# A fused attention and SwiGLU kernel: two pairs of heads transposed by DMA instead of TensorE

## The chip, the core and the metric

The kernel runs on one core of one Trainium2 chip. A core has a matrix engine (TensorE, "PE" in the profile; its weight loads are "PEld"), a vector engine (VectorE, "DVE"), an activation engine (ScalarE, "ACT"), a general engine (GpSimd, "POOL") and a queue engine (SyncE, "SP"). Each has its own instruction stream, and semaphores tie the streams together. Transfers run on 16 DMA engines; here GpSimd issues those that convert fp32 to fp16, and SyncE issues the others, the transposing ones among them. The metric is the device time of one execution in microseconds.

## The reference

Attention with a local window and a few global keys, followed by a gated feed-forward block. There are 4 batches, 8 heads, 768 positions and 64 values per head. Each query sees the first 8 keys and the last 96 keys up to itself.

```python
scores = scale * np.matmul(q, k.transpose(0, 1, 3, 2))
keep = is_global | is_local                 # first 8 keys, or 0 <= row - col < 96
scores = scores + bias[None, :, :, :]       # -slope of the head * distance
scores = np.where(keep, scores, -1000000000.0)
a = np.exp(scores - max); a = a / (sum(a) + 1e-09)
attn = np.matmul(a, v)                      # (4, 8, 768, 64)

x = attn.transpose(0, 2, 1, 3).reshape(3072, 512)
g = x @ w_gate                              # 512 x 1536
out = (g * sigmoid(g) * (x @ w_val)) @ w_out   # 1536 x 512
```

## The kernel before

The kernel works in fp16 with fp32 sums. A pair is two heads: four pairs in each batch, `hp` 0 to 3. A quad is two pairs: `g` 0 and 1. The feed-forward block runs over 8 tiles of 384 tokens, two for each batch; a tile has 12 steps `f`, one per 128 columns of the inner size. In each step there are four gate matmuls, four value matmuls and some output parts of three matmuls each (`out_part`; four parts make one 128 x 512 block of the output of the tile before). The attention of the coming batch is woven between these steps on TensorE.

For the scores, q and k have to lie with the head's 64 values on the partitions. Batch 1 gets this from TensorE:

```python
def transposes(self):                         # class Pair; batch 1, all four pairs
    trq, trk = (t[:, 0:S] for t in banks("trs", FP16))
    for st, tr in ((kst[b], trk), (qst[b], trq)):
        for j in range(J):                    # 6
            for hi in range(2):
                nc.tensor.transpose(...)      # 24 in all for a pair
    ...
    nc.scalar.copy(out=k3[...], in_=t3[...])  # two, PSUM to kT
    nc.vector.tensor_copy(out=self.qT..., in_=trq...)
    nc.vector.tensor_copy(out=k3[:, :, 0:NG], ...)   # the global keys, in every chunk
```

Batches 2 and 3 get it from DMA. Their q and k are loaded as rows (a position on each partition), the 8 global keys are put into partitions 0 to 7, and SyncE issues transposing transfers:

```python
def transposes_dma(self):
    for dst, st in ((self.kT[:, 0:S], kst), (self.qT, qst)):
        nc.sync.dma_start_transpose(out=..., in_=...)

def load_rows(b, i, h):                       # one head of q or k, on GpSimd's queue
    nc.gpsimd.dma_start(out=..., in_=src[b, h, 0:n * J].rearrange("(t p) d -> p t d", p=n))

def load_ends(b):                             # the last 48 keys of all heads, into kend
def turn_ends(b):                             # kE <- kend, one transposing transfer
    nc.sync.dma_start_transpose(out=kE, in_=kend[b].rearrange("p h d -> p (h d)"))
```

`kend` and `kE` have one buffer each. The seventh chunk of keys is read from `kE` where it was made by DMA.

The weighted values of a quad, and the scaling that gives x:

```python
def values(self, half, bank, mul_eng):        # class Quad; batch 1, first half
    den = bank("den"); self.weigh(half, den, None)
    for side in range(2):
        num = bank("num"); self.weigh(half, num, side)
        src = sb2.tile([128, TB], FP32, name="ns", tag="ns", bufs=4)
        nc.scalar.copy(out=src, in_=num[:, 0:TB])
    def scale_num(side):                      # xT block = ns * rb
        eng = mul_eng if side else nc.vector
        eng.tensor_mul(self.x_out(half, side), srcs[side], self.rb)
    def spread():
        self.spread()                         # rb <- dR
        if mul_eng is nc.gpsimd:
            scale_num(1)
    later.append(lambda: self.invert(den))    # dT <- den, dR <- dT, on VectorE
    later.append(spread)
    ...                                       # then scale_num for what is left
```

Entries of `later` are emitted one by one between the steps. A tile's gate and value products read four x blocks `xT[:, c, :]`, where block c is that of quad c // 2 and side c % 2.

The loads in GpSimd's stream, and the order of the steps in tile 1:

```python
stage(1)
load_qk(1, 0, 4)                              # pairs 0 and 1
load_globals()
load_wo(3)
load_qk(1, 4, 8)                              # pairs 2 and 3
for c in range(NCH):                          # V of batch 1, 7 chunks
    load_v_rest(1, c)
...
def va(b, g, half):
    return lambda: quads[b, g].values(half, bank, nc.vector)

def first(t, b):                              # (t, f): after step f; (t, f, n): before output part n
    return {(t, 2): [tr(b, 0), tr(b, 1)],
            (t, 4): [sc(b, (0, 0), (0, 1), (1, 0))],
            (t, 5): [tr(b, 2), tr(b, 3)],
            (t, 6): [sc(b, (1, 1), (2, 0), (2, 1))],
            (t, 8): [sc(b, (3, 0), (3, 1))],
            (t, 9): [va(b, 0, 0)],
            (t, 10, 1): [va(b, 1, 0), lambda: run_later(len(later))]}
...
# output parts after each step of tile 1, then tile 7
(ff(1, 0, 6, (1, 0, 0, 1, 1, 2)) + ff(1, 6, 10, (1, 1, 1, 0)) + ff(1, 10, 12, (2,)), first(1, 1)),
(ff(7, 0, 10, (1,)) + ff(7, 10, 12), {})
```

Of the kernel before, what the change touches and what calls it, by code (L numbers as in the profile page):

```python
# [10 lines left out]
FP16 = mybir.dt.float16  # L11
# [26 lines left out]
def kernel(  # L38
# [24 lines left out]
    J = S // 128  # L63
    NCH = 7
# [26 lines left out]
    sb2 = ctx.enter_context(tc.tile_pool(name="sb2", bufs=2))  # L91
# [62 lines left out]

    def stage_rows(b):
        qst[b] = sb2.tile([128, NP, J, 2, D], FP16, name="qst", tag="qst")
        kst[b] = sb2.tile([128, NP, J, 2, D], FP16, name="kst", tag="kst")
        kend[b] = sb2.tile([128, H, D], FP16, name="kend", tag="kend", bufs=1)
        nc.gpsimd.memset(kend[b], 0.0)
        nc.sync.dma_start(out=kend[b][0:NG], in_=kG[:, b - 1])  # L160
        for hp in range(NP):
            pair = kG[:, b - 1, 2 * hp:2 * hp + 2, :].rearrange("p h d -> p (h d)")
            nc.sync.dma_start(
                out=kst[b][0:NG, hp].rearrange("p t e d -> p t (e d)"),
                in_=pair.unsqueeze(1).broadcast_to([NG, J, 2 * D]))
# [17 lines left out]
    def copy_globals(b, c0=0):  # L183
        nc.sync.dma_start(
            out=vSs[b][0:NG, c0:],
            in_=vG[:, b, :, :].unsqueeze(1).broadcast_to([NG, NCH - c0, H, D]))


    def load_rows(b, i, h):
        st, src = ((qst, q), (kst, k))[i]  # L190
        p0, n = ((0, 128), (NG, KC))[i]
        nc.gpsimd.dma_start(  # L192
            out=st[b][p0:p0 + n, h // 2, :, h % 2, :],
            in_=src[b, h, 0:n * J].rearrange("(t p) d -> p t d", p=n))
# [58 lines left out]
    later = []  # L253

    def run_later(n):
        for _ in range(n):
            if later:
                later.pop(0)()

    class Pair:  # L260
# [114 lines left out]
        def scores(self, bk, mul_eng, sc):  # L375
            hp = self.hp
            for c in range(NCH):
                cb, col, q0, n = chunks[c]
                if cb != bk:
                    continue  # L380
                for hi in range(2):
                    r = slice(64 * hi, 64 * hi + 64)
                    keys = (kE[r, hp, :] if c == J and self.b > 1
                            else self.kT[r, 128 * c:128 * c + 128])
                    nc.tensor.matmul(  # L385
                        sc[hi][:, col:col + n], lhsT=keys,
                        rhs=self.qT[r, q0:q0 + n], start=True, stop=True)
            at = sb2.tile([128, 2, BANK], FP16, name="at", tag=f"at{bk}", bufs=NP)
            self.at[bk] = at

            def exps():
                for hi in range(2):
                    nc.scalar.activation(out=at[:, hi, :], in_=sc[hi][:, 0:BANK],  # L393
                                         func=AF.Exp, scale=scale)

            def mask():
                m = masks[:, 2 * hp:2 * hp + 2, :]
                if bk == 1:
                    for i in range(2):
                        a2 = at[:, :, WIN * i:WIN * i + WIN]  # L400
                        mul_eng.tensor_mul(a2, a2, m[:, :, WIN:2 * WIN])  # L401
                else:
                    o = WIN // 2 * bk
                    mul_eng.tensor_mul(at, at, m[:, :, o:o + BANK])  # L404

            return exps, mask

        def transposes_dma(self):
            b, hp = self.b, self.hp
            self.qT = sb2.tile([128, S], FP16, name="qT", tag="qT", bufs=NP)  # L410
            self.kT = kTs[hp]
            for dst, st in ((self.kT[:, 0:S], kst), (self.qT, qst)):
                nc.sync.dma_start_transpose(
                    out=dst.rearrange("r (t p) -> r t p", t=J),
                    in_=st[b][:, hp].rearrange("p t e d -> p (t e d)"))


    class Quad:
# [191 lines left out]
    quads = {(b, g): Quad(b, g) for b in range(B) for g in range(2)}  # L610
# [84 lines left out]
    load_qk(1, 0, 4)  # L695
    load_globals()
    load_wo(3)
    load_qk(1, 4, 8)
    for c in range(NCH):
        load_v_rest(1, c)  # L700

    gv["n"] = 1
    hb = [bank("gps") for _ in range(4)]
# [5 lines left out]
    def sc(b, *units):  # L709
        def step():  # L710
            for i, (hp, bk, *other) in enumerate(units):
                pair = pairs[b + 1 if other else b, hp]
                on_vector = pair.b < 2 or bk < 2 or hp % 2 == 0
                exps, mask = pair.scores(
                    bk, nc.vector if on_vector else nc.gpsimd,
                    [spare("sc") for _ in range(2)] if i == 0 and len(units) == 3
                    else banks("sc"))
                if i == 0:
                    exps()
                else:  # L720
                    later.append(exps)
                later.append(mask)
        return step

    def va(b, g, half):
        return lambda: quads[b, g].values(half, bank, nc.vector)

    def vas(b, half):
        return lambda: both_values(b, half)
# [1 line left out]
    def tr(b, hp):  # L731
        return pairs[b, hp].transposes
# [23 lines left out]
    def fetch(b, *hps):  # L756
        def step():
            for hp in hps:
                pairs[b, hp].transposes_dma()
            if hps[0] > 0:  # L760
                turn_ends(b)
        return step

    def first(t, b):
        return {(t, 2): [tr(b, 0), tr(b, 1)],
                (t, 4): [sc(b, (0, 0), (0, 1), (1, 0))],
                (t, 5): [tr(b, 2), tr(b, 3)],
                (t, 6): [sc(b, (1, 1), (2, 0), (2, 1))],
                (t, 8): [sc(b, (3, 0), (3, 1))],
                (t, 9): [va(b, 0, 0)],  # L770
                (t, 10, 1): [va(b, 1, 0), lambda: run_later(len(later))]}

    def both(t, b):

# [35 lines left out]
    def ff(t, f0, f1, n_out=(0,)):  # L810
        return [(t, f, n_out[(f - f0) % len(n_out)]) for f in range(f0, f1)]

    stretches = [
        (ff(0, 9, 10) + ff(0, 10, 12, (1,)), {}),
        (ff(1, 0, 6, (1, 0, 0, 1, 1, 2)) + ff(1, 6, 10, (1, 1, 1, 0)) + ff(1, 10, 12, (2,)), first(1, 1)),
        (ff(2, 0, 12, (1,)) + ff(3, 0, 12, (1,)), both(2, 1)),
        (ff(4, 0, 12, (1,)) + ff(5, 0, 12, (1,)), both(4, 2)),
        (ff(6, 0, 12, (1,)), second(6, 3)),
        (ff(7, 0, 10, (1,)) + ff(7, 10, 12), {})]

    loads, after = {}, {}
# [11 lines left out]
    for b, base, rate, v_at in ((2, 20, 2.0, (31, 32, 33, 34, 35, 36, 37)), (3, 38, 1.4, (56, 57, 58, 59, 60, 61, 62))):  # L833
# [105 lines left out]
```

The softmax here doesn't subtract the row's maximum and nothing guards it: scores larger than these inputs give would overflow.

## Time and profile before

| | before |
|---|---|
| median of 3 runs | 240.92 us (240.61 to 241.65) |
| span of the profiled run | 239.1 us |
| TensorE busy | 232.8 us (97%) |
| VectorE busy | 168.0 us (70%) |
| ScalarE busy | 127.7 us (53%) |
| GpSimd busy | 93.9 us (39%) |

In the page's busy table an engine is followed by its busy microseconds, the share of the span and the number of instructions. The slices divide the span into 40 equal parts of 5.98 us; a digit is the busy share in tenths, and 9 means 90% or more. In a list of waits a line gives who waited, for whom, the sum in us, how often, and the longest. In a timeline or a chain in order of time a line begins with the start in us and the duration in us. In the list of groups the columns are the line, the engine, the operation with its output and inputs, the shapes, the count, then busy us with the mean ns of one, then the engine's idle time before them and what ended it. "L272" is line 272 of the kernel before. SPq is SyncE's queue.

### The profile page before, as it was taken

What the parts mean: (1) busy time and instruction counts of PE and PEld (TensorE: products, weight loads), DVE (VectorE), ACT (ScalarE), POOL (GpSimd) and SP (SyncE); (2) the same over time, 40 slices, a digit from 0 to 9 for tenths busy, and PEclk for the clock granted to TensorE, in tenths of its full rate; (3) what the DMA queues carried; (4) which work ended last, traced back from release to release, by engine and by line L of the source; (5) the groups of instructions that cost most, each with busy time, mean ns of one, the idle gap of its engine ahead of it and who ended that gap; (6) DMA issues with size and microseconds to landing.
All of it is one profiled execution on the core that took longest, in us unless ns stands there. A gap on an engine that the chain in (4) does not pass through costs nothing.

```text
span 239.1 us, 6040 instructions
## 1 busy us (share of the span) xinstructions
PE 232.8 (97%) x2424; PEld 134.9 (56%) x2424; DVE 168.0 (70%) x363; ACT 127.7 (53%) x290; POOL 93.9 (39%) x113
## 2 busy tenths in 40 slices
PE   7899999999999999999999999999999999999994
PEld 4565565656555556555655556555655556555543
DVE  6889569978897678676885668776785668555530
ACT  4836776888846365367346365367356435233311
POOL 8976674568970003994082163700031213000000
PEclk9999999999999999999999999999999999999999
DMA  7999999999999446999149649920110110111022
GB/s 140 161 198 201 181 205 204 195 170 154 157 138 135 111 112 91 126 129 122 41 62 112 112 111 133 127 55 2 46 44 3 44 44 3 47 45 44 7 84 88
DMA packets 83332, 25.00 MB, mean 105 GB/s; under 512 B 72600, under 2 KB 80360, under 8 KB 83304
## 3 DMA queue, kind: packets, MB, share of 16 engines
q0 software_dynamic: 64208, 14.05, 64.2%
q1 hardware_dynamic: 18664, 10.36, 17.8%
q8 instruction: 19, 0.31, 0.5%
q10 hardware_dynamic: 432, 0.21, 0.4%
q14 instruction: 9, 0.07, 0.1%
HBM read 28.62 MB, written 6.29 MB: 146 GB/s over the span
## 4 chain that ended last, share of the span: by engine, by line
PE 85%; DMA 10%; POOL 3%; issue 1%; ACT 0%; POOLq 0%
PE ops L585 25%; PE gps L553 25%; PE vps L553 24%; DMA wg<-in_moe_w_gate_dram 10%; PE num L445 3%; PE sc L385 3%; PE den L445 2%; PE trs L272 1%; POOL vS L169 1%; PE ops L601 1%; POOL k L118 1%; POOL q L118 1%; POOL wg L211 0%; POOL vS L613 0%; ACT osb L605 0%
## 5 line engine op out<-in xcount | busy, mean ns | idle before, releaser
L564 ACT ACTIVATE th<-gps 128x384 f32<-128x384 f32 x96 | 47.3, 494 | 63.1 <-PE gps L553 57.3
L569 DVE SCALAR_TENSOR_TENSOR sl<-th,gps 128x384 f32<-128x384 f32 x96 | 52.7, 551 | 38.6 <-ACT th L564 38.0
L553 PE MATMUL gps<-xT,wg 128*128 128x384 f16 x384 | 78.2, 327 | 0.5 <-DVE xT L503 0.3
L553 PE MATMUL vps<-xT,wv 128*128 128x384 f16 x384 | 77.9, 326 | 0.2 <-DMA wv<-in_moe_w_val_dram 0.2
L585 PE MATMUL ops<-wo,hT 128*128 128x512 f16 x276 | 73.1, 379 | 0.0
L573 DVE TENSOR_TENSOR hT<-vps,sl 128x384 f16<-128x384 f32 x96 | 53.0, 554 | 8.2 <-PE vps L553 0.5
L553 PEld LDWEIGHTS <-wg 128*128 128x128 f16 x384 | 35.5, 98 | 32.1 <-issue 2.1
L553 PEld LDWEIGHTS <-wv 128*128 128x128 f16 x384 | 37.1, 98 | 25.6 <-DMA wv<-in_moe_w_val_dram 0.7
L585 PEld LDWEIGHTS <-hT 128*128 128x128 f16 x276 | 26.9, 98 | 23.6
L393 ACT ACTIVATE at<-sc 128x432 f16<-128x432 f32 x72 | 33.8, 534 | 10.2 <-PE sc L385 10.2
L522 POOL TENSOR_TENSOR xT<-ns,rb 128x384 f16<-128x384 f32 x10 | 9.8, 996 | 65.2 <-DVE rb L461 54.3
L169 POOL DMA_DIRECT2D vS<-in_v_dram x28 | 24.7, 891 | 5.5 <-DMA qst<-in_q_dram 1.4
L591 ACT ACTIVATE osb<-ops 128x512 f32<-128x512 f32 x23 | 13.7, 597 | 14.6 <-PE ops L585 14.4
L404 POOL TENSOR_TENSOR at<-at,masks 128x864 f16<-128x864 f16 x4 | 7.3, 1824 | 23.9 <-ACT at L393 19.3
L404 DVE TENSOR_TENSOR at<-at,masks 128x864 f16<-128x864 f16 x20 | 12.2, 609 | 5.6 <-ACT at L393 5.6
L192 POOL DMA_DIRECT2D kst<-in_k_dram x16 | 14.0, 897 | 2.2 <-PE sc L385 1.5
L518 ACT COPY ns<-num 128x384 f32<-128x384 f32 x24 | 9.8, 494 | 9.6 <-PE num L445 9.6
L192 POOL DMA_DIRECT2D qst<-in_q_dram x16 | 13.7, 883 | 0.9 <-DMA qst<-in_q_dram 0.6
L367 ACT ACTIVATE at<-sc 128x432 f16<-128x432 f32 (+2 forms) x32 | 11.4, 460 | 2.5 <-PE sc L356 2.5
L401 DVE TENSOR_TENSOR at<-at,masks 128x432 f16<-128x432 f16 x24 | 8.1, 377 | 4.4 <-ACT at L393 4.4
L445 PE MATMUL num<-at,vS 128*32 128x216 f16 (+6 forms) x576 | 10.9, 224 | 0.0
L455 DVE STREAM_TRANSPOSE dT<-den 128x384 f32<-128x384 f32 x16 | 9.3, 581 | 1.2 <-PE den L445 0.5
(71 smaller groups left out, 165.8 us busy)
## 6 DMA issues: line engine op xcount, KB each, us to landing
out_dram<-osb SPq DMA_DIRECT2D x23, 256.0 KB
vS<-in_v_dram POOLq DMA_DIRECT2D x24, 120.0 KB, 5.6
wg<-in_moe_w_gate_dram POOLq DMA_DIRECT2D x6, 256.0 KB, 7.7
wv<-in_moe_w_val_dram POOLq DMA_DIRECT2D x6, 256.0 KB, 8.1
wo<-in_moe_w_out_dram POOLq DMA_DIRECT2D x4, 384.0 KB, 10.3
qst<-in_q_dram POOLq DMA_DIRECT2D x16, 96.0 KB, 5.2
kst<-in_k_dram POOLq DMA_DIRECT2D x16, 90.0 KB, 5.6
kst<-in_k_dram POOLq DMA_DIRECT2D x2, 384.0 KB, 11.9
```

Of the source, the lines that this page charges most:

```text
L169: nc.gpsimd.dma_start(out=vSs[b][NG:NG + n, c, :, :], in_=v[b, :, KC * c:KC * c + n, :].rearrange("h p d -> p h d"))
L192: nc.gpsimd.dma_start(out=st[b][p0:p0 + n, h // 2, :, h % 2, :], in_=src[b, h, 0:n * J].rearrange("(t p) d -> p t d", p=n))
L367: nc.scalar.activation(out=at[:, hi, 0:col + n], in_=sc[hi][:, 0:col + n], func=AF.Exp, scale=scale)
L393: nc.scalar.activation(out=at[:, hi, :], in_=sc[hi][:, 0:BANK], func=AF.Exp, scale=scale)
L404: mul_eng.tensor_mul(at, at, m[:, :, o:o + BANK])
L445: nc.tensor.matmul(dst[r, o:o + n], lhsT=ones[:, 0:32] if side is None else vals[:, 4 * g + j, side::2], rhs=pairs[b, 2 * g + j // 2].at[c ...
L553: nc.tensor.matmul(gv[f, which][:, 0:TB], lhsT=w[:, c, 128 * f:128 * f + 128], rhs=x_of(t)[:, c, :], start=(c == 0), stop=(c == NC - 1))
L564: nc.scalar.activation(out=th, in_=dst[:, 0:TB], func=AF.Tanh, scale=0.5)
L569: nc.vector.scalar_tensor_tensor(out=sl, in0=th, scalar=1.0, in1=dst[:, 0:TB], op0=AluOp.add, op1=AluOp.mult)
L573: nc.vector.tensor_mul(hTs[t][:, f, :], dst[:, 0:TB], gv.pop(("sl", f)))
L585: nc.tensor.matmul(ops, lhsT=hTs[t][:, f, 128 * i:128 * i + 128], rhs=wo[:, f, :], start=(f == 0), stop=(f == NFF - 1))
L591: nc.scalar.mul(out=osb, in_=ops, mul=0.5)
```

## The change

Pairs 2 and 3 of batch 1 are transposed by DMA, as those of batches 2 and 3 are; pairs 0 and 1 stay on TensorE. For this their q and k are loaded as rows, one load for each head, and the first four chunks of V are issued between the rows of pair 2 and those of pair 3. The last three chunks of V are issued in tile 2. The steps behind the scores of pair 1 come one step later in tile 1. One output part moves from tile 7 to tile 1. In the first half of batch 1's values, GpSimd scales one of the two x blocks of a quad and VectorE the other. The change is meant to take work off TensorE and off the engines that emptied the transposes' PSUM banks. Helpers are renamed so that both ways can share one staging tile.

```diff
-    load_qk(1, 4, 8)
-    for c in range(NCH):
-        load_v_rest(1, c)
+    stage_ends(1)                       # kend: memset on GpSimd
+    for hp in range(2, NP):
+        for i in (1, 0):
+            for e in range(2):
+                load_rows(1, i, 2 * hp + e)
+        if hp == 2:
+            for c in range(4):
+                load_v_rest(1, c)
+    load_ends(1)
 ...
-        return lambda: quads[b, g].values(half, bank, nc.vector)
+        return lambda: quads[b, g].values(half, bank, nc.gpsimd)
 ...
-            if hps[0] > 0:
+            if hps[-1] == NP - 1:
                 turn_ends(b)
 ...
         return {(t, 2): [tr(b, 0), tr(b, 1)],
-                (t, 4): [sc(b, (0, 0), (0, 1), (1, 0))],
-                (t, 5): [tr(b, 2), tr(b, 3)],
-                (t, 6): [sc(b, (1, 1), (2, 0), (2, 1))],
-                (t, 8): [sc(b, (3, 0), (3, 1))],
-                (t, 9): [va(b, 0, 0)],
-                (t, 10, 1): [va(b, 1, 0), lambda: run_later(len(later))]}
+                (t, 4): [sc(b, (0, 0), (0, 1), (1, 0)), fetch(b, 2)],
+                (t, 5): [fetch(b, 3)],
+                (t, 7): [sc(b, (1, 1), (2, 0), (2, 1))],
+                (t, 9): [sc(b, (3, 0), (3, 1))],
+                (t, 10): [va(b, 0, 0)],
+                (t, 11, 1): [va(b, 1, 0), lambda: run_later(len(later))]}
 ...
-        (ff(1, 0, 6, (1, 0, 0, 1, 1, 2)) + ff(1, 6, 10, (1, 1, 1, 0)) + ff(1, 10, 12, (2,)), first(1, 1)),
+        (ff(1, 0, 6, (1, 0, 0, 1, 1, 2)) + ff(1, 6, 12, (1, 1, 1, 1, 1, 3)), first(1, 1)),
 ...
-        (ff(7, 0, 10, (1,)) + ff(7, 10, 12), {})]
+        (ff(7, 0, 12, (1, 1, 1, 0)), {})]
 ...
+    at_step(1, 0, lambda: rows_globals(1, 2))
     at_step(1, 7, lambda: [copy_globals(b) for b in range(1, B)])
+    at_step(2, 4, lambda: [load_v_rest(1, c) for c in range(4, NCH)])
-    ... batch 2's V chunks at steps (31, 32, 33, 34, 35, 36, 37)
+    ... batch 2's V chunks at steps (34, 35, 36, 37, 38, 39, 40)
```

(Cuts are marked by "..."; the last two lines shorten one long line of the kernel. Steps there are counted through the tiles, 12 to a tile. The cut parts are the renaming, and that the seventh chunk of keys is read from `kE` for pairs 2 and 3 of batch 1 too.)

More of the change, by code (lines that the diff above doesn't have):

```diff
@@ L155, in stage_rows, with stage_ends, rows_of, rows_globals @@
     def stage_rows(b):
-        qst[b] = sb2.tile([128, NP, J, 2, D], FP16, name="qst", tag="qst")
-        kst[b] = sb2.tile([128, NP, J, 2, D], FP16, name="kst", tag="kst")
+        stage(b)
+        stage_ends(b)
+        rows_globals(b, 0)
+    def stage_ends(b):
         kend[b] = sb2.tile([128, H, D], FP16, name="kend", tag="kend", bufs=1)
         nc.gpsimd.memset(kend[b], 0.0)
+    def rows_of(st, b, hp):
+        return st[b][:, 2 * hp:2 * hp + 2, :].rearrange("p h x -> p (h x)").rearrange(
+            "p (t e d) -> p t e d", e=2, d=D)
+    def rows_globals(b, hp0):
         nc.sync.dma_start(out=kend[b][0:NG], in_=kG[:, b - 1])
-        for hp in range(NP):
+        for hp in range(hp0, NP):
             pair = kG[:, b - 1, 2 * hp:2 * hp + 2, :].rearrange("p h d -> p (h d)")
             nc.sync.dma_start(
-                out=kst[b][0:NG, hp].rearrange("p t e d -> p t (e d)"),
+                out=rows_of(kst, b, hp)[0:NG].rearrange("p t e d -> p t (e d)"),
                 in_=pair.unsqueeze(1).broadcast_to([NG, J, 2 * D]))
@@ L192, in load_rows @@
         nc.gpsimd.dma_start(
-            out=st[b][p0:p0 + n, h // 2, :, h % 2, :],
+            out=rows_of(st, b, h // 2)[p0:p0 + n, :, h % 2, :],
             in_=src[b, h, 0:n * J].rearrange("(t p) d -> p t d", p=n))
@@ L382, in scores @@
                     r = slice(64 * hi, 64 * hi + 64)
-                    keys = (kE[r, hp, :] if c == J and self.b > 1
+                    keys = (kE[r, hp, :] if c == J and (self.b > 1 or hp > 1)
                             else self.kT[r, 128 * c:128 * c + 128])
@@ L414, in transposes_dma @@
                     out=dst.rearrange("r (t p) -> r t p", t=J),
-                    in_=st[b][:, hp].rearrange("p t e d -> p (t e d)"))
+                    in_=rows_of(st, b, hp).rearrange("p t e d -> p (t e d)"))
     class Quad:
@@ L831 @@
         mask_at(t, f, n % 2, n // 2, *((0, WIN), (WIN, 3 * WIN))[n % 2])
+    at_step(1, 0, lambda: rows_globals(1, 2))
     at_step(1, 7, lambda: [copy_globals(b) for b in range(1, B)])
-    for b, base, rate, v_at in ((2, 20, 2.0, (31, 32, 33, 34, 35, 36, 37)), (3, 38, 1.4, (56, 57, 58, 59, 60, 61, 62))):
+    at_step(2, 4, lambda: [load_v_rest(1, c) for c in range(4, NCH)])
+    for b, base, rate, v_at in ((2, 20, 2.0, (34, 35, 36, 37, 38, 39, 40)), (3, 38, 1.4, (56, 57, 58, 59, 60, 61, 62))):
         items = [(base, lambda b=b: stage_rows(b)), (base + 1, lambda b=b: load_ends(b))]
```

## The prediction

> **What bounds the kernel now.** I read the page first: busy shares, then the slices.
>
> ```profile
> PE 232.8 (97%) x2424; PEld 134.9 (56%) x2424; DVE 168.0 (70%) x363; ACT 127.7 (53%) x290; POOL 93.9 (39%) x113
> ...
> PE   7899999999999999999999999999999999999994
> ...
> PEclk9999999999999999999999999999999999999999
> DMA  7999999999999446999149649920110110111022
> ```
>
> TensorE is busy 97% of 239.1 us at full clock, and from the fourth slice on no slice is below 90%. A modelled busy share can hide pauses, so next I read who waited for whom on TensorE alone. All its listed waits come to 2.9 us, and all of them lie in the first part of the run:
>
> ```profile
> PE warm L621 <- DVE ones L126: 1.2, 1, 1.2
> PE trs L298 <- DMA q<-in_q_dram: 1.0, 2, 0.7
> PE gps L553 <- DVE xT L503: 0.3, 1, 0.3
> ```
>
> Third, TensorE's own timeline through tile 1: four-matmul groups start every 0.65 us without a gap. So the kernel is bound by the number of TensorE instructions, and only two things can move the time here: taking matmuls out, or making TensorE wait. The chain of work that ended last in order of time prices what goes:
>
> ```profile
> 53.01 1.29 PE ops L585 x6
> 54.30 1.46 PE trs L272 x48
> 55.77 0.76 PE gps L553 x4
> ```
>
> The 48 transposes of pairs 2 and 3 hold TensorE for 1.46 us (30 ns each), and the gate group after them takes 0.76 instead of 0.65.
>
> **What the Trainium skill says.** "TensorE: Matmul & The Clock Gate", Part 4: PE-mode transpose, says such a transpose lands in PSUM and needs a copy afterwards. The trace agrees: two vector copies of 0.95 us (L284) and ScalarE copies of 1.63 us (L280) follow each block. "DMA: Bandwidth & Descriptors", Issuing engines are not separate DMA queues, says transfers from all issuing queues interleave on the same 16 DMA engines; here the DMA line shows them 90% full in the slices where the new transposes must run. "PSUM — Partial Sum Buffer", Engine vs sequencer instructions, calls GpSimd's queue strictly FIFO; the trace agrees, every load and scaling starts in program order. "SBUF — State Buffer", SBUF: two separate sides, says a GpSimd operation and a vector operation with two SBUF inputs exclude each other for a whole instruction. The trace hints at it: the pair of vector scalings at 122.39 us takes 1.17 us where it overlaps GpSimd's scaling, but 1.03 us in the stretch after 200.92 us where the overlap is small.
>
> **Part 1, the transposes removed.** 1.46 + (0.76 - 0.65) = 1.57 us off TensorE. Two qT copies and two kT copies (about 2.2 us of VectorE with the small ones) and 1.63 us of ScalarE also go, in the stretch where VectorE is fullest (61.9 to 73.9 us). Output parts only move: one from tile 7 to tile 1, none added. With no new wait: 240.92 - 1.57 = 239.35 us.
>
> **Part 2, do pairs 2 and 3 arrive in time?** Their q and k now come as eight row loads of 90 or 96 KB in 256-byte source runs, in place of two loads of 384 KB. The GpSimd order of the new program is wo, memset, four row loads (pair 2), V chunks 0 to 3, four row loads (pair 3), ends. In the run before, the last wo was issued at 35.36 and landed 11.7 us later, at 47.1; the six full V chunks behind landed 1.0 us apart (issue plus landing: 52.0 to 57.1). One V chunk has 8 x 120 = 960 runs, a row load 720 to 768, so I estimate 0.8 us each. Pair 2 lands at 47.1 + 4 x 0.8 = 50.3; four V chunks bring 54.4; pair 3 lands at 57.6, and with some 1.5 us for the outputs and transposes that share the engines at 59. A DMA transpose holds its queue 1.2 to 1.3 us:
>
> ```profile
> 85.36 1.98 SPq L413 DMA_TRANSPOSE kT<-kst  x1
> 87.50 1.21 SPq L413 DMA_TRANSPOSE qT<-qst  x1
> 88.88 1.21 SPq L413 DMA_TRANSPOSE kT<-kst  x1
> 90.25 1.21 SPq L413 DMA_TRANSPOSE qT<-qst  x1
> 91.52 1.26 SPq L202 DMA_TRANSPOSE kE<-kend  x1
> ```
>
> Pair 2 is turned by about 54, pair 3 by about 61. When needed: after the outputs at 53.01 the gates of step 6 now start at 54.30; each step with one output part costs 1.95, so pair 2's scores come at 58.2 and pair 3's at about 63. Margins of 4 and 2 us: no wait expected. V's global rows wait on the same queue behind kE (61.3) and an output, so they land near 64; they are needed near 66.
>
> **Part 3, x for tile 2.** I expect the new wait here. The vector work before tile 2 was just in time before:
>
> ```profile
> 69.04 0.58 DVE L455 STREAM_TRANSPOSE dT<-den 128x384 f32<-128x384 f32 x1
> 69.66 0.23 DVE L456 RECIPROCAL dR<-dT 128x12 f32<-128x12 f32 x1
> 69.92 0.58 DVE L461 STREAM_TRANSPOSE rb<-dR 128x384 f32<-128x384 f32 x1
> 70.60 1.03 DVE L481 TENSOR_TENSOR xT<-ns,rb 128x384 f16<-128x384 f32 x2
> 71.55 0.55 DVE L569 SCALAR_TENSOR_TENSOR sl<-th,gps 128x384 f32<-128x384 f32 x1
> ```
>
> x was ready at 71.6 and tile 2's first gate group started at 71.44, whose fourth matmul needs the last x at 71.9. Between quad 1's numerators (end 68.2) and that group lay 3.25 us: an output part, step 11's two products, two output parts. In the new order quad 1 comes inside step 11, and only two output parts follow: 1.3 us. Let step 11's gates start at 0 (66.5 us on the clock). The outer groups then give: products 1.4, an output 0.65, denominators and numerators 0.9, two outputs 1.3, so tile 2's first gate starts at 4.3 and uses its four x blocks at 4.3, 4.45, 4.6, 4.75. VectorE: sl at 1.37 (as 82.08 to 83.45 shows), then rb, hT, x at steps of 0.41, 0.49, 0.44 and dT 0.46 later, at 3.2 (spacings of 66.78 to 69.04); dT to finished rb is 1.46, so 4.6. Then GpSimd scales one block in 1.0 us:
>
> ```profile
> L522 POOL TENSOR_TENSOR xT<-ns,rb 128x384 f16<-128x384 f32 x10 | 9.8, 996 | 65.2 <-DVE rb L461 54.3
> ```
>
> That ends at 5.75, 1.0 us after it is needed. If GpSimd and VectorE exclude each other, quad 0's vector scaling is held up 0.6 us and the final pair runs one after the other, up to 2.3 us late. I take 1.5.
>
> **Part 4, GpSimd's order.** The memset of kend for batch 2 must wait for kE of batch 1, since they share one buffer. Before, batch 2's rows were issued from 51.9; now from about 62. Nine loads at 0.85 fill GpSimd to about 70, and only then come the scalings, wanted at 68.9 and 71.2. So the first may be a little late; each us by which kE finishes after 62 also delays tile 2. Estimate: 0.3 us on average. Batch 2's first pairs land near 75, turned by 80, needed near 83; V chunks 4 to 6 land near 86, needed near 91. No wait.
>
> **Sum.** -1.57 + 1.5 + 0.3 = +0.2 us by this working. I choose 240.7 rather than 241.1: the part of 1.5 that rests on exclusion has only a 0.14 us hint in the trace.
>
> **Rivals.** (a) Everything is hidden: 239.3 us. For it: VectorE has lost some 3 us of work in this stretch, and GpSimd takes half of the scaling. Against: only 1.3 us of TensorE work is left behind quad 1. (b) The DMA side is late. The engines are already full from 48 to 58 us and I add small runs and five transposes there. If pair 3 lands 3 us later, its scores wait 1 us, V's global rows a similar time, and GpSimd reaches the scalings 2 to 3 us later: 242.5 to 244. Against: the last three V chunks leave that stretch. (c) GpSimd becomes the bound of tile 2's start, by the memset's wait alone: 241.5 to 242.5.
>
> **Range and chances.** Rival (a) sets the floor, 239.2. Working plus a 1 us delay of kE gives 242.1; I put the upper end at 242.5. To gain 2% would take 4.8 us, three times what is removed: 0.01. To lose 2%, new waits of 6.4 us: only (b) at its worst, 0.04. Within 2%: 0.95.
>
> **What would show each step.** Right: 48 fewer transposes and TensorE busy about 1.5 us less; no wait of the scores for the transposes; a TensorE wait of 1 to 2 us at the first gates of tile 2 for xT from POOL or DVE; batch 2's row loads issued from about 62. Wrong: no wait at tile 2 (a); a TensorE wait for kT, qT or vS near 58 to 66 (b); kE after 64 and GpSimd's first scaling after 72 (c). A wait later than 80 us for batch 2's kT or V would overturn Part 4.

## The result and the profile after

The changed kernel takes 248.58 us (median of 4 runs, 248.21 to 249.22), the kernel before 240.76 beside it: a ratio of 1.032, 95% interval 1.0283 to 1.0357. The prediction was 240.7 with a range up to 242.5.

On the page of the changed kernel, the busy shares and the slices (6.16 us each here):

```profile
PE 235.3 (96%) x2376; PEld 135.2 (55%) x2376; DVE 166.6 (68%) x357; ACT 125.8 (51%) x286; POOL 102.7 (42%) x123
...
PE   8899999999979969999999999999999999999994
...
PEclk9999999999997997999999999999999999999999
DMA  8999999999999995199917749690110110111022
```

TensorE has 48 instructions fewer and is busy 2.5 us longer. Two things are new in the slices: two dips of PE, and right at them two dips of the granted clock. The list of waits of TensorE names the first:

```profile
PE sc L394 <- DMA qT<-qst: 3.0, 2, 2.4
PE gps L562 <- DVE xT L490: 1.5, 1, 1.5
...
PE gps L562 <- POOL xT L490: 0.5, 1, 0.5
```

TensorE's timeline tells where they lie (the bracket is the idle time before, and what ended it):

```profile
59.07 0.55 PE L394 MATMUL sc<-qT,kT 64*128 64x216 f16 x8 [0.56 <-DMA qT<-qst]
...
71.55 0.49 PE L562 MATMUL gps<-xT,wg 128*128 128x384 f16 x2
73.58 0.32 PE L562 MATMUL gps<-xT,wg 128*128 128x384 f16 x1 [1.55 <-DVE xT L490]
74.42 0.32 PE L562 MATMUL gps<-xT,wg 128*128 128x384 f16 x1 [0.52 <-POOL xT L490]
...
91.06 0.36 PE L394 MATMUL sc<-qT,kT 64*128 64x216 f16 x4 [2.45 <-DMA qT<-qst]
```

So there are three places: pair 2 of batch 1 (0.56), the start of tile 2 (1.55 + 0.52, with 0.27 of idle time before 71.55), and pair 1 of batch 2 (2.45), in tile 2, whose scores the change doesn't touch. The windows behind the last two show the second effect; the columns are the stretch, its us, the busy time (and count) of PE, PEld, DVE, ACT and POOL, the granted clock, the time that DMA packets took as a mean of 16 engines, and GB/s:

```profile
74.90:78.80 3.90, 3.90 (x29) 1.94 (x27) 1.53 (x3) 1.82 (x4) 3.90 (x6) 0.56 1.16 73
91.20:95.70 4.50, 4.50 (x20) 2.08 (x17) 1.63 (x3) 2.18 (x5) 0.00 (x0) 0.62 1.08 184
```

The clock is at half for 3.41 us each time, from 75.08 and from 92.14 on, 0.7 and 1.1 us after TensorE resumes. The loss is (1 - 0.56) x 3.90 = 1.72 and (1 - 0.62) x 4.50 = 1.71 us.

Now a ledger. The denominators at step 8 of tile 2 start at 90.73 us before and at 98.98 after; one output part more (0.65) is done by then, so the changed kernel has lost 7.60 us up to there, and the spans differ by 7.3 in all.

| Term | us |
|---|---|
| transposes gone: from the outputs to step 6's gates, 52.85 to 55.70 before, 52.87 to 54.17 after | -1.55 |
| wait for qT, batch 1 pair 2 | 0.56 |
| start of tile 2 (0.27 + 1.55 + 0.52) | 2.34 |
| wait for qT, batch 2 pair 1 | 2.45 |
| half clock, twice | 3.43 |
| sum, of 7.60 measured | 7.23 |

The rest, 0.37, lies in how the waits are counted: a listed idle time is 0.2 to 0.3 us shorter than the delay that it makes here. From group start to group start, as in the first row, the three waits cost 0.74, 2.62 and 2.62 and the half clock 1.57 and 1.68, and the sum is 7.68. What made the waits is read from three other engines. SyncE's timeline, the transposes that those two waits for qT were for:

```profile
53.06 1.31 SPq L422 DMA_TRANSPOSE qT<-qst  x1
...
83.42 1.84 SPq L422 DMA_TRANSPOSE qT<-qst  x1
```

The first was issued at 53.06 and let the scores go at 59.07: 6.0 us. The second took from 83.42 to 91.06: 7.6 us. Before, the same transpose of batch 2 was issued at 78.16 and no packet moved from 82 to 84, so it took at most 3.8. GpSimd's timeline:

```profile
61.81 0.52 POOL L162 MEMSET kend<- 128x512 f16 x1 [9.15 <-DMA kE<-kend]
...
70.01 1.06 POOL L490 TENSOR_TENSOR xT<-ns,rb 128x384 f16<-128x384 f32 x1
73.00 1.37 POOL L490 TENSOR_TENSOR xT<-ns,rb 128x384 f16<-128x384 f32 x1 [1.94 <-DVE rb L470]
74.32 1.79 POOL L201 DMA_DIRECT2D kst<-in_k_dram  x2
...
81.12 2.56 POOL L178 DMA_DIRECT2D vS<-in_v_dram  x3
```

Behind the memset, row loads fill the engine to 69.96; then come the two scalings, and the other row loads and V of batch 2 stand behind them and are issued from 74.32 to 83.7. Batch 2's transposes are issued from 78.08 to 85.3, so both run together. And VectorE's timeline before tile 2:

```profile
69.79 1.70 DVE L490 TENSOR_TENSOR xT<-ns,rb 128x384 f16<-128x384 f32 x1
...
72.96 0.56 DVE L490 TENSOR_TENSOR xT<-ns,rb 128x384 f16<-128x384 f32 x1
```

One block of scaling takes 0.56 at 72.96, and 1.70 at 69.79: there GpSimd's scaling ran from 70.01 to 71.07. GpSimd's second scaling took 1.37 instead of 1.0, beside VectorE's of 72.96. The transposition that leads to quad 1's x (dT) came behind the 1.70, at 71.42.

### The profile page after: what moved, and what is told of

The parts are those of the page before. It is cut to its first block, busy times and chain, and to the rows that moved or that the text cites. A ratio compares the mean times of both kernels' runs of the same rounds, so it can differ in the third digit from the quotient of the medians.

```text
span 246.4 us, 5972 instructions
## 1 busy us (share of the span) xinstructions
PE 235.3 (96%) x2376; PEld 135.2 (55%) x2376; DVE 166.6 (68%) x357; ACT 125.8 (51%) x286; POOL 102.7 (42%) x123
## 4 chain that ended last, share of the span: by engine, by line
PE 84%; DMA 8%; DVE 3%; POOL 2%; issue 1%; ACT 1%; POOLq 0%; DVEq 0%; ACTq 0%
PE gps L562 25%; PE vps L562 24%; PE ops L594 22%; DMA qT<-qst 5%; PE sc L394 3%; PE num L454 3%; DMA q<-in_q_dram 2%; PE den L454 2%; PE sc L354 1%; PE ops L610 1%; PE sc L365 1%; DVE sl L578 1%; POOL k L118 1%; DVE xT L490 1%; DVE xT L512 1%
## 5 line engine op out<-in xcount | busy, mean ns | idle before, releaser
L562 PE MATMUL gps<-xT,wg 128*128 128x384 f16 x384 | 79.2, 329 | 2.5 <-DVE xT L490 1.5
L594 PE MATMUL ops<-wo,hT 128*128 128x512 f16 x276 | 74.5, 385 | 0.0
L402 ACT ACTIVATE at<-sc 128x432 f16<-128x432 f32 x72 | 33.2, 540 | 5.8 <-PE sc L394 5.8
L201 POOL DMA_DIRECT2D kst<-in_k_dram x20 | 17.5, 888 | 1.7 <-DMA wo<-in_moe_w_out_dram 1.6
L201 POOL DMA_DIRECT2D qst<-in_q_dram x20 | 17.1, 875 | 2.2 <-DMA wo<-in_moe_w_out_dram 1.1
L394 PE MATMUL sc<-qT,kT 64*128 64x216 f16 (+2 forms) x148 | 9.7, 259 | 3.0 <-DMA qT<-qst 3.0
```

Of the source, the lines that this page charges most:

```text
L201: nc.gpsimd.dma_start(out=rows_of(st, b, h // 2)[p0:p0 + n, :, h % 2, :], in_=src[b, h, 0:n * J].rearrange("(t p) d -> p t d", p=n))
L394: nc.tensor.matmul(sc[hi][:, col:col + n], lhsT=keys, rhs=self.qT[r, q0:q0 + n], start=True, stop=True)
L562: nc.tensor.matmul(gv[f, which][:, 0:TB], lhsT=w[:, c, 128 * f:128 * f + 128], rhs=x_of(t)[:, c, :], start=(c == 0), stop=(c == NC - 1))
L594: nc.tensor.matmul(ops, lhsT=hTs[t][:, f, 128 * i:128 * i + 128], rhs=wo[:, f, :], start=(f == 0), stop=(f == NFF - 1))
```

## The experiments

**The theory.** (1) A DMA transpose takes 6 us and more beside loads. (2) GpSimd's scalings stand in its own stream of loads, so they push batch 2's loads onto batch 2's transposes and, by exclusion, delay VectorE's scaling. (3) Waits of about 2 us cost as much again through the clock. **The rivals.** The memset of `kend` behind `kE` is what pushes the loads late, and GpSimd's scaling is harmless; or the transposes are late because of their place in SyncE's stream; or quad 1's late place in tile 1 explains the start of tile 2 alone. The part of (2) on the loads came only after the first four runs: the expectations of those blame exclusion for the scaling's cost and the memset for the late loads.

The medians of the kernel before, on the same chips: 240.62 us for the first four rows, 240.70 for the next four, 240.74 for the next three and 240.84 for the last. The ratio is estimated from the single runs and is not always the quotient of the medians.

| Run | us | ratio to before (95%) |
|---|---|---|
| changed kernel, scaling on VectorE | 242.38 | 1.0111 (1.0041 to 1.0181) |
| changed kernel, two kend buffers | 252.54 | 1.049 (1.0442 to 1.0538) |
| changed kernel, with useless matmuls | 247.15 | 1.0253 (1.0182 to 1.0323) |
| kernel before, GpSimd scaling alone | 244.01 | 1.0157 (1.01 to 1.0214) |
| changed kernel, all rows before the scalings | 245.74 | 1.0146 (1.0057 to 1.0236) |
| scaling on VectorE, quads early | 245.23 | 1.0172 (1.0099 to 1.0246) |
| one pair by DMA | 244.09 | 1.0125 (1.0067 to 1.0184) |
| kernel before, V loads beside the transposes | 247.16 | 1.0237 (1.0179 to 1.0296) |
| quads early, batch 2's scores later | 242.03 | 1.0055 (1.003 to 1.0081) |
| one pair, two kend buffers | 241.19 | 1.0024 (1.0008 to 1.0039) |
| the same, batch 2's scores later | 241.92 | 1.0042 (1.0025 to 1.0059) |
| both pairs, everything later | 241.28 | 1.0016 (1.0001 to 1.0031) |

**Scaling back on VectorE**, in the changed kernel:

```diff
-        return lambda: quads[b, g].values(half, bank, nc.gpsimd)
+        return lambda: quads[b, g].values(half, bank, nc.vector)
```

> The changed kernel, with batch 1's first-half x scaled by VectorE alone (GpSimd's half undone). Theory: GpSimd's scaling and VectorE's scaling of two on-chip inputs exclude each other, which held VectorE's first scaling for 1.2 us and GpSimd's second for 0.4 us. Without it the last x block comes some 1.0 us sooner, at about 73.4, the wait at tile 2 falls from 2.1 to 1.2-1.6 us, and the time to about 247.5; 246 if the wait gets too short to halve the clock. Rival: the late x comes from the place of quad 1 alone (two output parts behind it); then VectorE alone, with one more scaling per quad, is as late or later and the time is 248.6 or more. The wait of 2.4 us for batch 2's qT stays in both.

242.38 us, 1.8 above the kernel before, where the changed kernel is 7.8 above it: 6 us are back, more than the theory gave. The scalings gone, GpSimd's loads run on from 61.84 to 79 almost without a pause, and those that came from 74.32 on in the changed kernel are issued 4.6 to 5 us earlier; the wait for batch 2's qT is 0.63 instead of 2.45. The wait at tile 2 is 1.11, and in the profiled execution no stretch inside the kernel has half the clock (another run of it, 245.14 us, had a mean clock of 0.991). So one line of the change holds most of the loss. Why it is so much, the next runs had to tell.

**A second buffer for kend**, so that batch 2's rows needn't wait for `kE`:

```diff
-        kend[b] = sb2.tile([128, H, D], FP16, name="kend", tag="kend", bufs=1)
+        kend[b] = sb2.tile([128, H, D], FP16, name="kend", tag="kend", bufs=2)
```

> The changed kernel, with two buffers for kend in place of one, so that batch 2's memset and row loads no longer wait for batch 1's kE. Theory: the waits for batch 2's kT and qT (2.4 us, then 3.5 us at half clock) come from its rows still running on the DMA engines while its transposes do. With two buffers the rows are issued from about 53, the engines are free at 78, the wait and its half clock go: 248.6 - 2.4 - 1.7 = 244.5. Batch 1's pair 3 may get a wait of up to 1 us as the rows now run beside its transposes. Rival: the transposes are late because of their order on SyncE's queue and because kT is free only after tile 2's first scores; then they still start at 78, the wait stays and the time is 248 to 249.

252.54 us, 4 us worse than the changed kernel: the rival that blamed the memset, with GpSimd's scaling harmless, falls. The first rows now run from 53.56 to 62.4, beside the transposes of batch 1, and pair 2's scores wait 2.17 us for qT instead of 0.56. In GpSimd's timeline the engine then stands still:

```profile
73.26 1.00 POOL L490 TENSOR_TENSOR xT<-ns,rb 128x384 f16<-128x384 f32 x1 [10.82 <-DVE rb L470]
```

For 10.8 us no load is issued, though eight rows are left; they come from 77.52 on, and batch 2's wait grows to 3.02. The memset had kept loads off batch 1's transposes; the scalings keep them on batch 2's.

**Useless matmuls in the two long waits.** This kernel does more than the changed one: 36 matmuls of 256 columns whose results are overwritten, 16 ahead of tile 2's first gates and 20 ahead of the scores of batch 2's pair 1.

```diff
+            if (self.b, hp, bk) == (2, 1, 0):
+                dummies(sc[0], 20)
 ...
+        if (t, f, which, c0) == (2, 0, 0, 0):
+            dummies(gv[f, which], 16)
```

> The changed kernel, with matmuls that compute nothing of use put into TensorE's two long waits: 16 (of 256 columns) before tile 2's first gates, 20 before the scores of batch 2's pair 1, each into a bank that the real matmuls then overwrite. Theory: the clock is halved for 3.5 us because TensorE idled for 2 us or more; with the waits filled it stays at full speed and 1.5 to 1.7 us come back at each place: 248.6 - 3.2 = 245.4, although 36 matmuls were added and the x and qT arrive no sooner. Rival: the clock drop is a limit that has nothing to do with the idle time (power, or the work after it); then the half clock stays, and the time is 248.6 or up to 0.5 above.

The same two windows in the profiled execution of this kernel (245.44 us, against 248.21 of the changed kernel's):

```profile
74.90:78.80 3.90, 3.90 (x37) 2.36 (x37) 2.65 (x6) 3.65 (x9) 3.90 (x6) 1.00 1.39 142
91.20:95.70 4.50, 4.50 (x27) 2.47 (x26) 3.29 (x7) 3.01 (x7) 0.00 (x0) 1.00 1.20 173
```

The clock stays at 1.00, and in the first stretch VectorE and ScalarE finish 6 and 9 operations instead of 3 and 4. With more to do, the kernel is 2.8 us faster in this execution: the half clock was a cost of its own and not a mark of the waits. Other runs of it took 245.57, 248.72 and 251.26 us, with mean clocks of 1.0, 0.993 and 0.985, and 0.993 is some 1.7 us lost, so the filling did not always keep the clock. Waits of 1.6 us for qT and 0.3 for x are left.

**GpSimd's scaling alone**, in the kernel before:

```diff
-        return lambda: quads[b, g].values(half, bank, nc.vector)
+        return lambda: quads[b, g].values(half, bank, nc.gpsimd)
```

> The kernel before, with the one part that GpSimd scales half of x in batch 1's first half; transposes, loads and places as before. Theory (exclusion): VectorE's scaling is held while GpSimd's 1.0 us one runs, x for tile 2 comes about 1 us later than 71.6, its first gates wait 0.7 to 1.2 us, and the time is 241.5 to 242. Rival: the scalings run side by side and VectorE is relieved of two operations of 0.5 us; x is ready no later and the time stays at 240.8.

244.01 us: this line alone costs 3.4 us where nothing else is changed. GpSimd's timeline:

```profile
67.90 1.00 POOL L481 TENSOR_TENSOR xT<-ns,rb 128x384 f16<-128x384 f32 x1 [9.44 <-DVE rb L461]
...
72.15 1.73 POOL L192 DMA_DIRECT2D qst<-in_q_dram  x2
```

The engine stands 9.4 us for rb with ten row loads behind it. They are issued from 72.15 to 80.7, beside batch 2's transposes (74.18 to 80.5), and the scores wait 3.10 us for qT. At tile 2 there is only 0.17 us of wait. So the scaling costs here through the loads that it holds back, hardly through x.

**All rows before the scalings**, in the changed kernel, by two kend buffers and a higher rate of batch 2's row loads:

```diff
-tag="kend", bufs=1)
+tag="kend", bufs=2)
 ...
-    for b, base, rate, v_at in ((2, 20, 2.0, ...
+    for b, base, rate, v_at in ((2, 20, 8.0, ...
```

> The changed kernel with two kend buffers, and with all 16 row loads of batch 2 ahead of GpSimd's two scalings in its stream (GpSimd still scales). New theory: not kE's memset but the scalings held up the loads, since GpSimd works in order and waited for VectorE's rb; eight row loads and three V loads behind them then ran beside batch 2's transposes. Here the rows are issued from about 53 to 70, so the 3.0 us wait of the two-buffer run for batch 2's qT falls below 0.6 with no half clock behind it. Batch 1's qT stays late by about 2.2 us (its transposes now run beside those rows), and tile 2 stays late by about 2.1 us through exclusion: about 248. Rival: batch 2's qT is late for its place on SyncE's queue; then it stays late by 2.4 to 3 us and the time near 252.

245.74 us. The wait for batch 2's qT is gone from the list, as the theory says; SyncE's stream is the same, so the rival that blamed its order falls. But now the row loads from 52.98 on run beside batch 1's transposes, and pair 2's scores wait 3.01 us. The start of tile 2 keeps its waits (0.30, 0.86, 0.53), since both engines still scale. (The profiled execution was one of the slower ones, 247.31 us, and is read only for where the waits lie.)

**Quads early**: scaling on VectorE, and the values of quads 0 and 1 two steps and one substep earlier (the global rows of V too):

```diff
+                (t, 8): [va(b, 0, 0)],
-                (t, 10): [va(b, 0, 0)],
-                (t, 11, 1): [va(b, 1, 0), lambda: run_later(len(later))]}
+                (t, 11, 0): [va(b, 1, 0), lambda: run_later(len(later))]}
 ...
+    at_step(1, 1, lambda: copy_globals(1))
```

> The vector-scaling version with quad 0's values three places earlier (after step 8), quad 1's before all three output parts of step 11, and V's global rows of batch 1 copied at step 1. If the place of quad 1 and the vector chain behind it set the rest of tile 2's wait (1.1 us there), that wait falls to 0.3 or less, and the time from 242.4 to about 241.0. The waits for batch 1's qT (0.4) and batch 2's qT (0.6) stay. Rival: tile 2 waits for something else than the vector chain (V, or TensorE's own order); then it stays at 1.1.

245.23 us, 4 more than expected. The wait at tile 2 is gone, so the late place of the quads, without GpSimd, is worth the 1.11 us seen in the first experiment. But batch 2's qT is 2.53 late: `kE` was ready 1.4 us later than there (memset at 62.69 against 61.27), so the last rows and V were issued 1.1 us later, beside transposes issued at the same times as there (76.0 to 82.8). The last of these took 7.1 us from issue to the scores (81.21 to 88.34) instead of 4.9 (81.54 to 86.44). The wait is 1.9 us more than there; the rest is in part clock, at a place that the edit does not touch: in the profiled execution TensorE ran at half clock from 7.96 to 11.37, after a wait of 1.32 us for q, and the mean clocks of the four runs were 0.985 to 0.993.

**One pair by DMA**: pair 3 only, scaling on VectorE, the steps, output parts and V order as before, but for V's global rows, which are copied at step 1 as with quads early.

```diff
-                (t, 5): [tr(b, 2), tr(b, 3)],
+                (t, 4): [..., fetch(b, 3)],
+                (t, 5): [tr(b, 2)],
```

(against the kernel before; pair 3's q and k are loaded as rows)

> Only pair 3 of batch 1 by DMA, pair 2 on TensorE, scaling on VectorE, the steps of tile 1 and the output parts where the kernel before had them, all V chunks of batch 1 in their old place. 24 transposes go: 0.73 us off TensorE, and with pair 2 on TensorE nothing waits at the scores of pairs 1 and 2; tile 2 is as in time as before. If the theory (late transposes and the scaling's side effects are all that the change lost) is right: 240.6 - 0.7 = 239.9, at most 240.4 if batch 2's rows, which still wait for kE, cost some 0.5 us. If something else in DMA transposes in tile 1 costs time: 241 or more.

244.09 us. Even one pair needs `kE`, so the memset of batch 2 still waits to 61.79, the rows run to 76.7 beside transposes from 73.21 on, and the scores wait 2.90 us. TensorE then ran at half clock from 88.17 to 91.58. So the memset does matter where no scaling stands in the stream.

**V loads beside the transposes**, in the kernel before and nothing else: the V chunks of batches 2 and 3 are issued early, at one step.

```diff
-    for b, base, rate, v_at in ((2, 20, 2.0, (31, 32, 33, 34, 35, 36, 37)), (3, 38, 1.4, (56, ...
+    for b, base, rate, v_at in ((2, 20, 2.0, (31, 31, 31, 31, 31, 31, 31)), (3, 38, 1.4, (31, ...
```

> The kernel before, with nothing changed but the time of V's loads: the rest of batch 2's and all of batch 3's V are issued from 70 to 81 us, beside the transposes of batch 2's pairs 0 and 1, which then had idle DMA engines. If loads on the DMA engines alone make a transpose take 6 us in place of some 2, the scores of batch 2's pair 1 (needed 84.5, last transpose issued near 79) wait 0.5 to 3 us for qT, and the time is 241.5 to 245. If transposes are slow for another reason: no wait, 240.6.

247.16 us, 6.5 more, from the place of 14 loads that were early enough before. SyncE's timeline, and then TensorE's, of this kernel:

```profile
78.56 2.37 SPq L413 DMA_TRANSPOSE qT<-qst  x1
```

```profile
87.92 0.54 PE L385 MATMUL sc<-qT,kT 64*128 64x216 f16 x4 [3.85 <-DMA qT<-qst]
```

The transpose is issued 0.40 us later than before and takes 9.4 us. The windows tell what differs: first the kernel before, then this one.

```profile
82.00:84.00 2.00, 2.00 (x13) 0.98 (x10) 1.16 (x3) 0.49 (x1) 0.00 (x0) 1.00 0.00 0
```

```profile
82.00:84.00 2.00, 2.00 (x19) 0.96 (x17) 1.17 (x3) 0.86 (x2) 0.00 (x0) 1.00 2.22 131
```

Before, all is over by 82 us. Here more than one packet is open on a DMA engine on average (2.22 us of packets in 2.00 us). The granted clock was at half from 86.42 to 93.24, twice as long as elsewhere; from 87.92 on that costs 2.66 us, and with the wait of 3.85 it makes up the 6.5. This is the cleanest proof of point (1): same transposes, same order on SyncE, only loads beside them.

**Batch 2's scores later**: quads early, and the first scores of batch 2's pairs after step 7 of tile 2 instead of step 5.

```diff
-                (t, 5): [sc(b, (3, 2), (0, 0, n), (1, 0, n)), fetch(n, 2, 3)],
+                (t, 5): [sc(b, (3, 2)), fetch(n, 2, 3)],
+                (t, 7): [sc(b, (0, 0, n), (1, 0, n))],
```

> Both pairs by DMA, scaling on VectorE, quad 0 early as in the run before, and batch 2's first scores (pairs 0 and 1) two steps later in tile 2, after step 7 instead of step 5: some 3.9 us more for their transposes, which still run beside the row loads. If late transposes are what is left of the loss, the wait of 2.5 us for batch 2's qT goes, 0.4 us at batch 1's pair 2 stays, and the time is 240.6 - 1.57 + 0.5 + some tenths = 239.5 to 240.2, below the kernel before. If the loads make the transposes later still, or something else is lost, 241 or more.

242.03 us. The wait of 2.53 is gone: two steps of TensorE work hide the slow transpose. What is left is pair 2 of batch 1, 2.08 us late for its scores at 60.18.

**One pair, two kend buffers**, and **the same with batch 2's scores later** (the two edits shown above, on the kernel with one pair):

> The one-pair version with two kend buffers, so that batch 2's row loads start at about 54 in place of 62 and are through before its transposes at 73, as in the kernel before. The wait of 2.9 us for batch 2's qT goes; pair 3 of batch 1 is needed at 62 and its transposes, issued from 52, now run beside more loads, but with 8 us to spare. 240.6 - 0.73 + 0.1 = 239.9 to 240.2. If pair 3 waits now, or batch 2's qT still does: 241 or more.

> The one-pair version with two kend buffers and batch 2's first scores two steps later as well. If the two-buffer version already has no wait, this one is the same, 239.9 to 240.2; if that one still waits for batch 2's qT, this one is faster by that wait.

241.19 and 241.92 us. With one pair, the second buffer does take away batch 2's wait: no scaling stands in the queue. Some 0.75 us of transposes are saved, and pair 3 waits 0.74 us; the list of waits names a copy of global keys for it, which does not settle what was late. In the second kernel pair 3 waits 0.60 us for qT, and the later scores bring nothing.

**Both pairs, everything later**: the kernel of "batch 2's scores later", with pair 1's second half alone after step 7, pair 2's scores after step 9, the last after step 10, quad 1 at the second place of step 11, and one output part moved from tile 2 into step 11 of tile 1 to cover it.

```diff
-                (t, 7): [sc(b, (1, 1), (2, 0), (2, 1))],
+                (t, 7): [sc(b, (1, 1))],
-                (t, 9): [sc(b, (3, 0), (3, 1))],
-                (t, 11, 0): [va(b, 1, 0), lambda: run_later(len(later))]}
+                (t, 9): [sc(b, (2, 0), (2, 1), (3, 0))],
+                (t, 10): [sc(b, (3, 1))],
+                (t, 11, 1): [va(b, 1, 0), lambda: run_later(len(later))]}
```

> Both pairs by DMA, VectorE scaling, and everything that a DMA transpose feeds placed later: batch 1's pairs 2 and 3 are scored after step 9 (needed at about 62 in place of 58), quad 0's values after step 8, quad 1's before the second of four output parts of step 11 (one part moved there from step 11 of tile 2), batch 2's first scores after step 7 of tile 2. If late transposes and the vector chain at tile 2 are all that is lost, every wait is now below 0.4 us and the time is 240.74 - 1.57 + 0.5 = 239.7, below the kernel before. If pair 3's qT (landing near 61 to 62) or batch 1's backlog of exponentials and masks makes TensorE wait by 1 us or more: 240.5 to 242, and then the freed 1.57 us cannot be kept in this order of loads.

241.28 us: every wait over 0.3 us that the change had made is gone, and the gain doesn't come. TensorE's timeline, the start of tile 2:

```profile
71.92 1.33 PE L562 MATMUL gps<-xT,wg 128*128 128x384 f16 x4
73.08 0.81 PE L562 MATMUL vps<-xT,wv 128*128 128x384 f16 x4
```

The four gate matmuls hold 1.16 us up to the values, where such a group takes 0.65: 0.51 of pauses between single matmuls, which the list of waits doesn't show. The denominators at 68.66 take 0.64 up to the next group instead of 0.29 (as at 70.01 of the kernel with all rows first), and a score group at 63.23 takes 0.87 where 12 such matmuls took 0.66 at 50.90 of the changed kernel. The four of the last score group take 0.47 at 66.14, where four took 0.29 at 57.92, and the values at 98.76 come 1.10 after their gates instead of 0.65, of which the list shows 0.28 (for sl). That makes 1.70. The removed transposes freed 1.55 and this kernel is 0.44 above the one before, so some 0.3 us more went that was not assigned; it has more changes between kinds of matmul groups, but no run priced these. No version here beats the kernel before.

## Why the prediction was wrong, point by point

**Right: the saving and the bound.** The transposes were worth 1.57 by the prediction and 1.55 in the timeline. The time is still moved by TensorE's work and its waits, and by its clock, which the sum left out. One reading was wrong: the vector copies that went had run from 55.15 to 57.35, and not in the stretch from 61.9 to 73.9, so they gave no room just ahead of tile 2.

**Part 2, half wrong.** Pair 2's transposes were issued before 54.4, as said, but "turned by about 54" took the 1.3 us for which a transpose holds its queue for its landing. It landed 6.0 us after its issue, at 59.07, and cost 0.56. This mistake recurs in Part 4, where it weighs more.

**Part 3, right in kind, too small.** The wait at tile 2's first gates, for xT from VectorE and GpSimd, came as described: 2.34 against 1.5 taken and 2.3 named as the upper bound with exclusion. (By the working's own terms GpSimd's scaling ends at 4.6 + 1.0 = 5.6 and not at 5.75, so 0.9 us late and not 1.0; the error is small beside what was missed.) The exclusion that the 0.14 us hint stood for is real: 1.70 instead of 0.56 for a vector scaling beside GpSimd's. With the scaling on VectorE 1.11 is left, and with the quads earlier nothing. So about half belongs to the late place of the quads and half to GpSimd; the split is an estimate, as those kernels differ in their loads too.

**Part 4, the step that failed.** "Batch 2's first pairs land near 75, turned by 80, needed near 83 ... No wait." The first half held: memset at 61.81 (predicted 62), rows to 69.96 (70), scalings late. But the prediction asked only whether the scalings would be late for TensorE and not what stood behind them in the same stream. Rows and V of batch 2, held to 74.32, ran beside batch 2's transposes. The last of these needed 7.6 us; between its issue (83.42) and the time at which its scores were wanted (91.06 - 2.45 = 88.61) lay 5.2. Up to the start of the whole score group the slack was 6.0 us before (78.16 to 84.12) and 4.6 after (83.42 to 88.06); the landing took at most 3.8 before. The same wait appears in the kernel before from GpSimd's scaling alone (3.10) or from V loads alone (3.85), and goes when the loads are put elsewhere. The sentence on what would make the prediction wrong, a wait later than 80 us for batch 2's kT or V, comes within a name of this event (it was qT, of the same pair); the chances gave it no weight.

**The missing term, the clock.** The sum took waits as if a microsecond of idle time cost a microsecond. Two waits of about 2.4 us cost another 3.4. "TensorE: Matmul & The Clock Gate", Part 1: The HAM clock gate, says the clock is 4/8 or 8/8, set by windows of about 3.4 us that run free of the program. The trace agrees in the two values (0.50 and 1.00), in the length (3.41 us at half) and in that the windows run on by themselves, as the starts below show. It does not support reading this as a demand for a whole idle window of 3.4 us before the clock falls: here it fell after 1.55 + 0.52 and after 2.45 us of waiting.

**The rivals.** (c) saw the place at tile 2 and (b) saw late DMA, but at 58 to 66 us and for pairs 2 and 3 of batch 1. Neither looked at batch 2. With the sum of the four new terms, 0.56 + 2.34 + 2.45 + 3.43 = 8.8, the prediction's 239.35 becomes 248.1.

**What stays open.** Which wait halves the clock is settled in part. Of the ten waits of 1.8 us or more seen in the profiles of the changed kernel and the experiments (that with all rows first left aside), seven were followed by half clock (the changed kernel's two, three with two kend buffers, one pair's 2.90, the V loads' 3.85), and three were not (3.10, 2.53, 2.08). Of those up to 1.6 us one was, the 1.32 for q with quads early. The traces explain most of this. Within an execution the half clock begins only on a grid of 3.41 us: in the changed kernel at 75.08, five steps later at 92.14, and 45 steps later, when all matmuls are done, at 245.74. What the drops go with is the idle time of TensorE within one cell of the grid. Two cells of the changed kernel, and then two with GpSimd's scaling alone, whose grid is read from its one start, at 243.34, when all matmuls are done:

```profile
71.66:75.08 3.42, 1.35 (x8) 0.58 (x7) 1.69 (x4) 0.29 (x1) 2.08 (x2) 1.00 0.87 77
75.08:78.49 3.41, 3.41 (x25) 1.66 (x24) 1.23 (x3) 1.64 (x4) 3.41 (x5) 0.50 1.16 73
```

```profile
82.91:86.33 3.42, 2.03 (x19) 0.92 (x17) 1.55 (x4) 1.93 (x4) 0.52 (x1) 1.00 1.85 169
86.33:89.74 3.41, 1.70 (x13) 1.03 (x14) 0.27 (x2) 0.55 (x2) 0.00 (x0) 1.00 2.05 198
```

In the first pair, 3.42 - 1.35 = 2.07 us idle fall into one cell, and the next cell is at half. In the second pair, a boundary splits the 3.10 us into 1.39 and 1.71, and the clock stays. The other two waits that were not followed are split as well (2.53 into 0.66 and 1.87, 2.08 into 1.56 and 0.52); of the seven that were, six have 2.0 us or more in one cell and one has 1.84. Between 1.5 and 1.9 both happen (followed: 1.51 and 1.84), and that stays open; so does the cause, since no run moved a wait against the grid. Nor did any run tell whether number, size or bytes of the loads slow a transpose.

## What to carry to other kernels

A compute operation put on the engine that also issues loads must be judged by what stands behind it in that stream, and where those loads then run. Take a DMA transpose's time from issue to the release of its reader, under the traffic it will meet, not from how long it holds the queue. On a TensorE that is otherwise never idle, count a new wait of about 2 us or more as possibly double.

## What the runs showed of the hardware that was not expected

- A DMA transpose of 128 x 768 fp16 within SBUF took at most 3.8 us from its issue with little beside it, and 4.9 to 9.4 us beside loads (the last of two or four in a row, what stood ahead of it in the queue included); its hold on the queue was 1.2 us before and 1.2 to 2.4 us in these. "DMA: Bandwidth & Descriptors", Queues, rings and completion order, says each DMA engine takes turns between its queues packet by packet, which fits; the packets themselves were not studied.
- The granted clock fell to half for 3.41 us, once for twice that, after seven of ten TensorE waits of 1.8 to 3.9 us; in the changed kernel each cost 1.7 us. Within an execution it fell only on a grid of 3.41 us, and inside the kernel it did so whenever 2.0 us or more of idle time lay in the cell before (six cases, 2.00 to 3.01). Matmuls with no use, put into the wait, kept it at 1.00 in the profiled execution.
- A vector scaling with two SBUF inputs took 1.70 and 1.20 us beside GpSimd's, instead of 0.56, and GpSimd's took 1.37 instead of 1.00.
